# Moving memory scores behind a projection bank, and copies from VectorE to ScalarE, in a fused two-layer recurrent-memory kernel

## The chip, the cores and the metric

The kernel runs on one core of one Trainium2 chip. The metric is the device time of one execution in microseconds (us). Engines are called by their names or by their short forms in the profile: PE is TensorE (PEld its weight loads), DVE is VectorE, ACT is ScalarE, POOL is GpSimd, SP is SyncE.

## The reference

Two rounds of a segment-recurrent attention layer with memory tokens and a gated feed-forward layer, on 2048 tokens of width 448, in bfloat16:

```python
def _A_ref(x, mem0, Wq, Wk, Wv, Wo, seg_len):     # 64 segments of 32 tokens, 16 heads of 256
    mem = mem0                                    # 8 memory tokens
    for s in range(n_seg):
        h = concat([mem, x[:, s*seg_len:(s+1)*seg_len]], axis=1)   # 40 rows
        q, k, v = h@Wq, h@Wk, h@Wv
        scores = where(mask, q@k.T * Dh**-0.5, -1e9)
        o = (softmax(scores) @ v) @ Wo
        mem = o[:, :M]                            # the next segment's memory
        outs.append(o[:, M:])
    return concat(outs, axis=1)

def _B_ref(x, W_gate, W_up, W_down):
    gate, up = x@W_gate, x@W_up
    return (gate * (gate > 0) * up) @ W_down

x = A_x
x = x + _A_ref(layernorm(x), ...);  x = x + _B_ref(layernorm(x), ...)
x = x + _A_ref(layernorm(x), ...);  x = x + _B_ref(layernorm(x), ...)   # the same weights
```

## The kernel before, in words

**Folded weights.** A first part folds Wq with Wk and Wv with Wo for each head into resident tables, `A_sb` and `B_sb`. After it a head's scores are (h A) h' and its output (P h) B; keys and values are the rows of h themselves.

**Steps.** `step(g, ...)` is called for g = 0 to 68. It works on segment g of the first attention round (chain 0) and on segment g - 4 of the second one (chain 1) at the same time; both are active in steps 4 to 63. The two halves of the heads (hf 0 and 1, 8 heads each) go through it one behind the other. Every second step (g odd, from 3) also carries one block of feed-forward work, an object of class `Feed`, `ff`. I call a step with `ff` a long one and a step without it a short one.

**What a step does for a half.** `project` computes h A for 28 tiles of 128 columns, in five banks of PSUM, the on-chip memory of 8 banks that TensorE writes (`BANKS`: first tile and number of tiles; those at 0, 6, 12 and 18 have six tiles, that at 24 has four, and its upper and lower 64 partitions belong to different tiles). The copies out of the banks at 0, 6, 12 and 18 go to `TQ`, that at 24, the split bank, to `TZ` in two halves. In the profile these banks are `prj`. A quarter of the products of the four full banks is issued beforehand by `project_early`, so that 18 are left of each. `scores_m` computes the scores of the memory tokens' queries (bank `Sm`), `scores_x` those of the segments' own tokens (bank `Sx`); each sums over four parts of the width (kd 0 to 3: kd 0 and 1 read the TQ tiles 0 to 15, kd 2 the tiles 16 to 23, kd 3 reads TZ) and returns two functions from `softmax`. The first of them issues on VectorE the maximum (`mx`) and the difference (`se`) and on ScalarE the exponential; the second the sum (`ssum`), its reciprocal and the product, which gives `PM` or `PX`. `flipped` transposes those on TensorE (`pps`) and copies the result to SBUF (`PT`). `weigh_m` (banks `ya`, `yb`) and `weigh_x` (banks `y`) multiply it with h, held in `hk`, and copy to `Y`. `project_out` and `project_last` multiply Y by `B_sb` into `ox` and `o`; memory rows go back into h (`hT`) for the next step. The weigh_x of half 1 is called in the next step, through `late`.

**Order.** TensorE's instructions are issued in program order, and from the first step on so are VectorE's and ScalarE's (class `InOrder`). A planner, `bank`, gives every PSUM tile the bank that is free soonest by an estimate of time that it keeps while the program is written; a bank's new products wait for the last reader of its old ones.

**Around the change**, in a step with both chains, TensorE's order is: late weigh_x of half 1 of the step before (`y`), Sm of half 0, half 1's banks 0, 6, 24, 12, in a long step the transpose for the feed-forward layer (`tps`), bank 18, the flip of PM, Sx of half 0, `ya` and `yb` of half 0, Sm and Sx of half 1. A long step goes on with the gate and up products (`gate_up(u)`, u = 0 to 6: banks `ups` and `gps`, ScalarE's copy `ut`, VectorE's product `hh`; `ut` has two buffers), between which the flips of half 1's PM and half 0's PX stand, and with the down product (`down`). `ff.residual` and `ff.norm` add the residual (`xa`) and normalise (`xn`) on VectorE while half 0 is projected.

Of the kernel before, what the change touches and what calls it, by code (L numbers as in the profile page):

```python
# [40 lines left out]

BANKS = ((0, 6), (6, 6), (24, 4), (12, 6), (18, 6))
EARLY = (((0, 6), (12, 18)), ((0, 6), (12, 18)))


def upper(hf, t):

    return any(b <= t < b + 6 for _, b in EARLY[hf])

# [6 lines left out]
def build_kernel(ctx, tc, A_x, A_mem0, A_Wq, A_Wk, A_Wv, A_Wo, B_W_gate, B_W_up, B_W_down, out,  # L56
                 ntiles=16, nseg=64):
    nc = tc.nc
    P = nc.NUM_PARTITIONS
# [15 lines left out]
    def in_order(r):  # L75
        if last_pe[0] is not None:
            tc.add_manual_dep(r.ins, last_pe[0],
                              mybir.DependencyInfo(mybir.DependencyClass.NoSync,
                                                   mybir.DependencyReason.DATA),
                              reason="order of issue")  # L80
        last_pe[0] = r.ins.name
# [22 lines left out]
    dve, act = InOrder(nc.vector), InOrder(nc.scalar)  # L104
# [16 lines left out]
    def let_go(t):  # L121

        i, after = bank_of[t.name]
        held.discard(i)
        free_at[i] = now[0] + after
# [7 lines left out]
    def mm(out, lhsT, rhs, **k):  # L133
        in_order(nc.tensor.matmul(out, lhsT, rhs, **k))  # L134
        n = 1
        for d in out.shape[1:]:
            n *= d
        pair = lhsT.shape[0] <= 64 or lhsT.shape[-1] == 64 and out.shape[0] == 64
        passed(out, max(25, n / 2.4 + 2.5) * (0.5 if pair else 1))
# [5 lines left out]
    def evac(eng, dst, src):  # L145
        if eng is act:
            act.copy(dst, src)
        else:
            eng.tensor_copy(dst, src)
# [54 lines left out]
    TQ, TZ, YB, PX, PM = [], [], [], [], []  # L204
# [51 lines left out]
    with tc.tile_pool(name="pre", bufs=6) as pre:  # L256
# [71 lines left out]
        for p in range(NP):  # L328
            hf, p4 = divmod(p, 4)
# [31 lines left out]
        for p in range(NP):  # L361
            hf, p4 = divmod(p, 4)
# [4 lines left out]
            for eo in range(2):  # L367
                for kd in range(3):
                    bps = bank([P, 512], F32, "bps")
                    for t in range(2):  # L370
                        e = 2 * eo + t
                        mm(bps[:, 0:DM], vT[:, e, kd * 128:(kd + 1) * 128], wo[:, e, :],
                           start=(t == 0), stop=(t == 1))
# [4 lines left out]
            for t in range(2):  # L378
                for eo in range(2):
                    e = 2 * eo + t  # L380
                    mm(bps[64 * eo:64 * eo + 64, 0:DM], vT[:, e, 384:448], wo[:, e, :],
                       start=(t == 0), stop=(t == 1), tile_position=(0, 64 * eo))
# [115 lines left out]
    def moving(hb, j, idx, chains, rows=slice(0, P)):  # L498

        if len(chains) == 2:  # L500
            return hb[rows, j, idx * HI:(idx + 1) * HI].rearrange("p (c k) -> p c k", k=64)[:, :, 0:L]
        c = chains[0]
        return hb[rows, j, idx * HI + 64 * c:idx * HI + 64 * c + L]

    def project_early(hf, chains, hb, j):

        n = L * len(chains)
        pre = {}
        for pair in EARLY[hf]:
            for i0 in pair:  # L510
# [4 lines left out]
                       moving(hb, j, 3, chains, rows), start=(i == 0), stop=False, skip_group_check=True)  # L515
        return pre

    def project(hf, chains, hb, j, banks, pre={}, busy=False):

        n = L * len(chains)  # L520
        for i0, k in banks:
            ps = pre[i0] if i0 in pre else bank([P, 512], F32, "prj")
            for i in range(k):
                for kd in range(3 if i0 in pre else 4):
                    mm(ps[:, i * n:(i + 1) * n], A_sb[:, kd, hf, i0 + i, :], moving(hb, j, kd, chains),
                       start=(kd == 0 and i0 not in pre), stop=(kd == (2 if i0 in pre else 3)),
                       skip_group_check=i0 in pre)
            if i0 in pre:
                let_go(ps)
            if i0 < 24:  # L530
                T = TQ[hf][:].rearrange("p g u w -> p g (u w)")[:, :, 16 * i0:16 * (i0 + k)]
                parts = [(act if i0 % 12 or busy and hf and i0 else dve, slice(0, P), T)]
            else:
                parts = [(dve, slice(0, 64), TZ[hf][0:64, :, 0:64]),
                         (act, slice(64, 128), TZ[hf][64:128, :, 64:128])]
            for eng, rows, T in parts:
                T = T.rearrange("p g (t q) -> p t g q", q=16)
                if len(chains) == 2:
                    evac(eng, T, ps[rows, 0:k * n].rearrange("p (t g q) -> p t g q", t=k, q=16))
                    continue  # L540
                c = chains[0]
                src = ps[rows, 0:k * n].rearrange("p (t w) -> p t w", t=k)
                x, m = (0, SEG) if c == 0 else (MEM, 0)
                evac(eng, T[:, :, 2, MEM * c:MEM * c + MEM], src[:, :, m:m + MEM])
                evac(eng, T[:, :, 3 * c:3 * c + 2, :],
                     src[:, :, x:x + SEG].rearrange("p t (g q) -> p t g q", q=16))

    def queries(hf, g, kd):
        return TQ[hf][:, g, 2 * kd:2 * kd + 2, :] if kd < 3 else TZ[hf][:, g, :]
# [23 lines left out]

        return first, second

    def flipped(src, n, tag):
        pps = bank([P, n, 128], BF, "pps")
        for b in range(n):
            tr(pps[:, b, :], src[:, 2 * b:2 * b + 2, :], ident[:])
        PT = main.tile([P, n * 128], BF, tag=f"PT{tag}", name="PT")  # L580
        dve.tensor_copy(PT[:], pps[:].rearrange("p b q -> p (b q)"))
        return PT

    def active(g):
# [2 lines left out]
    def step(g, ff, pre, late):  # L587
        chains = active(g)
        xs = active(g - 1)
        ms = [c for c in chains if g - c * LAG + 1 < nseg]  # L590
        gb, j = divmod(g, BLK)
        hb = hTb[gb % 2]
# [22 lines left out]
        def scores_m(hf):  # L615
            if not ms:
                return (lambda: None,) * 2
            Sp = bank([P, 2, L], F32, "Sm", 1100)
            for kd in range(4):
                mm(Sp[:, :, :], queries(hf, 2, kd), moving(hb, j, kd, (0, 1)), start=(kd == 0), stop=(kd == 3))  # L620
            return softmax(Sp, 2, PM[hf], blk[:], f"m{hf}")

        def scores_x(hf):
            Sp = bank([P, 4, L], F32, "Sx", 2500 if hf == 0 else 3500 if ff is None else 8000)
            both = len(chains) == 2
            if not both:
                mm(Sp[:, :, :], ident[:], maskS[:], start=True, stop=False, skip_group_check=True)
            for half in range(2):
                for c in chains:
                    for kd in range(4):  # L630
                        mm(Sp[:, 2 * half + c, :], queries(hf, 3 * c + half, kd), moving(hb, j, kd, (c,)),
                           start=(both and kd == 0), stop=(kd == 3), skip_group_check=True)
            return softmax(Sp, 4, PX[hf], None, f"x{hf}", maskS[:] if len(chains) == 2 else None)

        def weigh_m(hf, hk, PT):
# [115 lines left out]
        if ff is not None:  # L751
            ff.residual()
        next_piece()
        project(0, chains, hb, j, BANKS[2:5], pre)
        if ff is not None:
            ff.norm()
        pre1 = {}
        if late is not None:
            pre1 = project_early(1, chains, hb, j)
            late()  # L760
        m0 = scores_m(0)
        m0[0]()
        project(1, chains, hb, j, BANKS[0:2], pre1)
        m0[1]()
        next_piece()
        project(1, chains, hb, j, BANKS[2:4], pre1, ff is not None)
        if ff is not None:
            ff.xposed()
        project(1, chains, hb, j, BANKS[4:5], pre1)
        pm = flipped(PM[0], 1, "m0") if ms else None  # L770
        x0 = scores_x(0)
        weigh_m(0, hk, pm)
        m1 = scores_m(1)
# [3 lines left out]
        if ff is not None:  # L777
            feed(0)
            m1[1]()
            feed(1)  # L780
            x0[1]()
            feed(2, 3)
            next_piece()
            pm = flipped(PM[1], 1, "m1") if ms else None
            feed(4)
            px0 = flipped(PX[0], 2, "x0")
            weigh_m(1, hk, pm)
            feed(5, 6)
            x1[0]()
            x1[1]()  # L790
            ox_open()
            project_out(0, 0, 8)
            next_piece()
            ff.down()
            ff.norm2()
            project_out(0, 8, NT)
            project_last()
            next_piece()
            project_out(1, 0, 12)
            px1 = flipped(PX[1], 2, "x1")  # L800
            ff.feed_on()
            project_out(1, 12, NT)
        else:
            next_piece()
            ox_open()
            m1[1]()
            x0[1]()
            project_out(0, 0, 23)
            pm = flipped(PM[1], 1, "m1") if ms else None
            project_out(0, 23, NT)  # L810
            px0 = flipped(PX[0], 2, "x0")
            weigh_m(1, hk, pm)
            x1[0]()
            next_piece()
            x1[1]()
            project_last()
            project_out(1, 0, 22)
            px1 = flipped(PX[1], 2, "x1")
            next_piece()
            project_out(1, 22, NT)  # L820
# [3 lines left out]
        pre = project_early(0, nxt, hTb[(g + 1) // BLK % 2], (g + 1) % BLK) if nxt else {}  # L824
# [7 lines left out]
    pre, late = {}, None  # L832
    for g in range(nsteps + 1):
# [3 lines left out]
        pre, late = step(g, Feed(i) if g % 2 and 0 <= i < nblk + LAG // BLK - 1 else None, pre, late)  # L837

    ff = Feed(nblk + LAG // BLK - 1)
# [64 lines left out]
```

## Time and profile before

| | |
|---|---|
| time, median of 3 runs | 1670.48 us (1670.42 to 1671.86) |
| time of the profiled execution | 1672.79 us |
| its span, first to last instruction | 1671.0 us |
| mean granted TensorE clock | 0.994 |
| busy: TensorE, VectorE, ScalarE | 97%, 73%, 41% |
| HBM traffic over the span | 15 GB/s |

The profile is that of one execution. Instructions are grouped by engine, operation and tile name; nearly all are issued through one helper for each kind of engine, so they share a few line numbers (L134 are matrix products and their weight loads, L142 transposes, L92 the instructions of VectorE and ScalarE), and the tile names tell them apart. A row of the order of time has start, duration, engine, operation, `out<-in`, and in brackets the idle time ahead of it with what ended it. Ends of products are modelled, since they overlap in the array.

### The profile page before, as it was taken

How to read it: one execution, taken by the hardware profiler on the slowest of the kernel's cores; microseconds unless marked ns; L12 is line 12 of the kernel's file. 1: busy time of each engine (PE TensorE's matmuls, PEld its weight loads, DVE VectorE, ACT ScalarE, POOL GpSimd, SP SyncE). 2: the span in 40 equal slices, each digit the busy share in tenths (PEclk: the TensorE clock that was granted, in tenths of full speed). 3: DMA queues.
4: the chain of work that ended last, by engine and by line, in shares of the span. 5: the costliest groups of instructions: out<-in, count | busy, mean ns of one | idle time of the engine just before them, and what ended most of it. 6: DMA issues, size and time to landing. Idle time of an engine off the chain costs nothing.

```text
span 1671.0 us, 90168 instructions
## 1 busy us (share of the span) xinstructions
PE 1614.8 (97%) x41152; PEld 1485.6 (89%) x41152; DVE 1212.2 (73%) x3984; ACT 689.0 (41%) x1998; POOL 90.9 (5%) x178
## 2 busy tenths in 40 slices
PE   8999999999999999999999999999999999999997
PEld 6698899999999899999999999999999999999886
DVE  7776777777777777777777777777777777777775
ACT  5733443444334434443344344433443344433432
POOL 6200000000000000000000000000000000000000
PEclk9989999999999999999999999999999999999999
DMA  9430000000000000000000000000000000000000
GB/s 253 129 108 15 8 9 9 4 9 9 9 9 9 9 9 6 7 9 9 9 9 9 9 9 4 9 9 9 9 9 9 9 4 9 9 7 7 6 6 6
DMA packets 26783, 33.16 MB, mean 20 GB/s; under 512 B 3352, under 2 KB 24736, under 8 KB 26400
## 3 DMA queue, kind: packets, MB, share of 16 engines
q1 hardware_dynamic: 25312, 23.70, 5.3%
q8 instruction: 322, 5.28, 1.3%
q0 software_dynamic: 1088, 3.68, 0.7%
q14 instruction: 61, 0.50, 0.1%
HBM read 23.70 MB, written 1.84 MB: 15 GB/s over the span
## 4 chain that ended last, share of the span: by engine, by line
PE 85%; DVE 7%; ACT 4%; POOL 2%; issue 1%; POOLq 0%; ACTq 0%; DVEq 0%
PE prj L134 24%; PE ox L134 24%; PE ups L134 6%; PE dps L134 5%; PE gps L134 5%; PE o L134 5%; PE Sx L134 3%; PE y L134 3%; ACT Y L92 2%; PE Sm L134 2%; PE ya L134 2%; PE bps L134 1%; DVE stats L92 1%; PE pps L142 1%; ACT TQ L92 1%
## 5 line engine op out<-in xcount | busy, mean ns | idle before, releaser
L134 PE MATMUL prj<-hT,A_sb 128*128 128x80 bf16 (+3 forms) x15232 | 530.2, 199 | 0.2 <-issue 0.2
L134 PEld LDWEIGHTS <-A_sb 128*128 128x128 bf16 (+1 forms) x15232 | 493.8, 99 | 16.2 <-issue 0.9
L134 PEld LDWEIGHTS <-B_sb 128*128 128x128 bf16 (+1 forms) x15232 | 491.1, 103 | 14.0 <-issue 0.4
L134 PE MATMUL ox<-Y,B_sb 128*128 128x80 bf16 (+4 forms) x11424 | 435.9, 199 | 0.4 <-issue 0.4
L92 DVE CAST Y<-y 128x256 bf16<-128x256 f32 (+2 forms) x400 | 160.9, 457 | 66.2 <-PE y L134 66.2
L92 ACT CAST TQ<-prj 128x480 bf16<-128x480 f32 (+1 forms) x340 | 162.2, 498 | 86.6 <-PE prj L134 84.6
L92 ACT ACTIVATE se<-se 128x80 f32<-128x80 f32 (+1 forms) x270 | 81.9, 303 | 212.2 <-DVE se L92 212.2
L92 DVE CAST TQ<-prj 128x480 bf16<-128x480 f32 (+2 forms) x268 | 150.1, 569 | 6.3 <-PE prj L134 5.7
L134 PEld LDWEIGHTS <-hk 40*128 40x128 bf16 (+1 forms) x1950 | 105.6, 96 | 44.7 <-issue 31.9
L134 PE MATMUL ups<-xT,Wu_sb 128*128 128x128 bf16 (+1 forms) x1904 | 140.8, 217 | 1.9 <-DVE hh L92 1.3
L134 PE MATMUL gps<-xT,Wg_sb 128*128 128x128 bf16 (+1 forms) x1904 | 140.9, 218 | 0.0
L92 ACT CAST Y<-y 128x256 bf16<-128x256 f32 (+1 forms) x368 | 129.6, 418 | 20.5 <-PE y L134 16.5
L92 DVE SCALAR_TENSOR_TENSOR hh<-gps,ut 128x256 bf16<-128x256 f32 (+1 forms) x238 | 93.8, 406 | 59.7 <-PE gps L134 53.2
L92 ACT CAST ut<-ups 128x256 bf16<-128x256 f32 (+1 forms) x238 | 81.8, 358 | 89.0 <-DVE hh L92 52.7
L134 PEld LDWEIGHTS <-Wu_sb 128*128 128x128 bf16 x1904 | 111.2, 99 | 2.4 <-issue 2.4
L134 PEld LDWEIGHTS <-Wg_sb 128*128 128x128 bf16 x1904 | 112.7, 99 | 0.0
L134 PEld LDWEIGHTS <-TQ 128*128 128x128 bf16 x1938 | 86.8, 97 | 27.4 <-issue 11.8
L92 DVE COPY PT<-pps 128x128 bf16<-128x128 bf16 (+1 forms) x270 | 68.7, 254 | 49.5 <-PE pps L142 48.1
L134 PE MATMUL y<-PT,hk 40*128 40x256 bf16 (+1 forms) x1280 | 99.3, 248 | 4.0 <-ACT Y L92 0.6
L218 POOL TENSOR_SCALAR rstd<-mv 128x1 f32<-128x1 f32 x67 | 14.8, 221 | 1516.2 <-DVE mv L92 1516.2
L92 ACT CAST TZ<-prj 64x320 bf16<-64x320 f32 (+2 forms) x152 | 55.9, 378 | 98.7 <-DVE TZ L92 96.5
L134 PE MATMUL dps<-Wd_sb,hh 128*128 128x448 bf16 x476 | 96.2, 354 | 0.0
(117 smaller groups left out, 1924.9 us busy)
## 6 DMA issues: line engine op xcount, KB each, us to landing
wo<-in_A_Wo_dram POOLq DMA_DIRECT2D x8, 448.0 KB, 5.7
nat<-in_A_Wq_dram SPq DMA_DIRECT2D x8, 384.0 KB, 6.1
nat<-in_A_Wk_dram SPq DMA_DIRECT2D x8, 384.0 KB, 5.6
nat<-in_A_Wv_dram SPq DMA_DIRECT2D x8, 384.0 KB, 5.0
xa<-in_A_x_dram SPq DMA_DIRECT2D x32, 56.0 KB, 2.2
xa<-xp SPq DMA_DIRECT2D x32, 56.0 KB, 1.9
out_dram<-xa SPq DMA_DIRECT2D x32, 56.0 KB, 2.3
xp<-in_A_x_dram SPq DMA_DIRECT2D x30, 56.0 KB, 2.6
```

Of the source, the lines that this page charges most:

```text
L92: r = f(*a, **k)
L134: in_order(nc.tensor.matmul(out, lhsT, rhs, **k))
L142: in_order(nc.tensor.transpose(out, src, idn))
L218: nc.gpsimd.tensor_scalar(out=rstd[:], in0=mv[:, 1:2], scalar1=EPS, scalar2=None, op0=ALU.add)
```

## The change

Five edits, all in the steps:

1. In a step, half 0's `scores_m` and the first part of its softmax come behind half 1's first bank (the bank at 0) instead of ahead of it. The second part of that softmax is issued between the products of the bank at 6 and the copy out of it (`first`), instead of behind that copy.
2. In long steps both halves of the split bank (24) are copied by ScalarE, for both halves of the heads; before, VectorE took one.
3. In long steps, of half 1's banks the one at 0 is copied by ScalarE and the one at 6 by VectorE; before it was the other way round. Those at 12 and 18 stay on ScalarE.
4. In long steps the flip of half 1's PM and that of half 0's PX are copied by ScalarE instead of VectorE.
5. The scores sum over kd in the order 0, 1, 3, 2, so that the part that reads the bank at 18 comes last.

```diff
+KD = (0, 1, 3, 2)
...
-    def project(hf, chains, hb, j, banks, pre={}, busy=False):
+    def project(hf, chains, hb, j, banks, pre={}, busy=False, first=None):
...
             if i0 in pre:
                 let_go(ps)
+            if first is not None:
+                first()
             if i0 < 24:
...
-                parts = [(act if i0 % 12 or busy and hf and i0 else dve, slice(0, P), T)]
+                parts = [(act if (i0 != 6 if busy and hf else i0 % 12) else dve, slice(0, P), T)]
             else:
-                parts = [(dve, slice(0, 64), TZ[hf][0:64, :, 0:64]),
+                parts = [(act if busy else dve, slice(0, 64), TZ[hf][0:64, :, 0:64]),
                          (act, slice(64, 128), TZ[hf][64:128, :, 64:128])]
...
-    def flipped(src, n, tag):
+    def flipped(src, n, tag, eng=dve):
...
-        dve.tensor_copy(PT[:], pps[:].rearrange("p b q -> p (b q)"))
+        evac(eng, PT[:], pps[:].rearrange("p b q -> p (b q)"))
...
-            for kd in range(4):
-                mm(Sp[:, :, :], queries(hf, 2, kd), moving(hb, j, kd, (0, 1)), start=(kd == 0), stop=(kd == 3))
+            for kd in KD:
+                mm(Sp[:, :, :], queries(hf, 2, kd), moving(hb, j, kd, (0, 1)), start=(kd == KD[0]), stop=(kd == KD[-1]))
...
-        project(0, chains, hb, j, BANKS[2:5], pre)
+        project(0, chains, hb, j, BANKS[2:5], pre, ff is not None)
...
+        project(1, chains, hb, j, BANKS[0:1], pre1, ff is not None)
         m0 = scores_m(0)
         m0[0]()
-        project(1, chains, hb, j, BANKS[0:2], pre1)
-        m0[1]()
+        project(1, chains, hb, j, BANKS[1:2], pre1, ff is not None, m0[1])
         next_piece()
         project(1, chains, hb, j, BANKS[2:4], pre1, ff is not None)
         if ff is not None:
             ff.xposed()
-        project(1, chains, hb, j, BANKS[4:5], pre1)
+        project(1, chains, hb, j, BANKS[4:5], pre1, ff is not None)
...
-            pm = flipped(PM[1], 1, "m1") if ms else None
+            pm = flipped(PM[1], 1, "m1", act) if ms else None
             feed(4)
-            px0 = flipped(PX[0], 2, "x0")
+            px0 = flipped(PX[0], 2, "x0", act)
```

More of the change, by code (lines that the diff above doesn't have):

```diff
@@ L629, in scores_x @@
                 for c in chains:
-                    for kd in range(4):
+                    for kd in KD:
                         mm(Sp[:, 2 * half + c, :], queries(hf, 3 * c + half, kd), moving(hb, j, kd, (c,)),
-                           start=(both and kd == 0), stop=(kd == 3), skip_group_check=True)
+                           start=(both and kd == KD[0]), stop=(kd == KD[-1]), skip_group_check=True)
             return softmax(Sp, 4, PX[hf], None, f"x{hf}", maskS[:] if len(chains) == 2 else None)
```

## The prediction

> **What bounds the kernel now.** I read the page first (busy shares), then the waits, the stretches of one pair of steps, and the order of time of that pair on four engines.
>
> The page's engine row, the list of waits (engine line waited for: us in total, times, longest) and the table by stretch (a step without feed-forward work, here a short step, then one with it, a long step):
>
> ```profile
> PE 1614.8 (97%) x41152; PEld 1485.6 (89%) x41152; DVE 1212.2 (73%) x3984; ACT 689.0 (41%) x1998; POOL 90.9 (5%) x178
> ...
> PE ya L134 <- DVE PT L92: 14.2, 37, 0.6
> PE Sm L134 <- ACT Y L92: 13.3, 36, 0.4
> ...
> 719.53:738.12 18.59, 18.19 (x532) 17.54 (x530) 14.14 (x48) 7.96 (x23) 0.00 (x0) 1.00 0.01 4
> 738.12:766.98 28.86, 28.21 (x668) 25.82 (x667) 20.63 (x66) 11.51 (x33) 1.58 (x4) 1.00 0.05 11
> ```
>
> TensorE, in order, is the bound: 97% busy, clock 1.00, 18.59 us for a short step and 28.86 us for a long one. Only its pauses can be won, and there are few. Two have a name: it waits some 36 times for ScalarE's copy out of a bank (Sm <- ACT Y) and 37 times for VectorE's copy of a flip (ya <- DVE PT), about 0.4 us each. VectorE is 76% busy in a short step (14.14 of 18.59), 71% in a long one; ScalarE 40%.
>
> Where these pauses lie in a short step (start us, us, engine, what; the bracket is idle time and its releaser):
>
> ```profile
> 724.54 0.65 PE L134 MATMUL y<-PT,hk 40*128 40x256 bf16 x10
> 725.59 0.27 PE L134 MATMUL Sm<-hT,TQ 128*128 128x80 bf16 x3 [0.40 <-ACT Y L92]
> 725.73 3.32 PE L134 MATMUL prj<-hT,A_sb 128*128 128x80 bf16 x88
> 728.89 0.22 PE L142 MATMUL pps<-ident,PM 128*128 128x128 bf16 x1
> 729.42 0.27 PE L134 MATMUL ya<-PT,hk 128*128 128x128 bf16 x2
> 724.96 1.03 ACT L92 CAST Y<-y 128x512 bf16<-128x512 f32 x3 [0.20 <-PE y L134]
> 726.67 0.27 ACT L92 ACTIVATE se<-se 128x80 f32<-128x80 f32 x1 [0.68 <-DVE se L92]
> 724.99 1.22 DVE L92 CAST Y<-y 128x512 bf16<-128x512 f32 x3 [0.77 <-PE y L134]
> 726.13 0.23 DVE L92 TENSOR_REDUCE mx<-Sm 128x2 f32<-128x80 f32 x1
> 726.39 0.24 DVE L92 TENSOR_TENSOR se<-Sm,mx 128x80 f32<-128x80 f32 x1
> 726.58 0.66 DVE L92 CAST TQ<-prj 128x480 bf16<-128x480 f32 x1
> 727.16 0.23 DVE L92 TENSOR_REDUCE ssum<-se 128x2 f32<-128x80 f32 x1
> 728.44 0.66 DVE L92 CAST TQ<-prj 128x480 bf16<-128x480 f32 x1
> 729.14 0.23 DVE L92 COPY PT<-pps 128x128 bf16<-128x128 bf16 x1
> ```
>
> Sm takes the bank that the first y product used, and waits until ScalarE has emptied it. But VectorE, from its first Y copy at 724.99 to the flip's copy at 729.14, has no bracket: it works through without a pause, and ya comes right behind that copy. So this 0.40 us of TensorE is nearly covered by VectorE.
>
> The same place in a long step, and its second half:
>
> ```profile
> 742.34 0.45 DVE L92 CAST TZ<-prj 64x320 bf16<-64x320 f32 x1
> 742.88 0.42 ACT L92 CAST TZ<-prj 64x320 bf16<-64x320 f32 x1 [1.01 <-DVE TZ L92]
> 743.32 0.56 ACT L92 CAST TQ<-prj 128x480 bf16<-128x480 f32 x1
> 743.35 0.96 PE L134 MATMUL y<-PT,hk 40*128 40x256 bf16 x10
> 743.93 0.20 PEld L134 LDWEIGHTS <-hk 40*128 40x128 bf16 x4 [0.37 <-issue]
> 744.46 0.27 PE L134 MATMUL Sm<-hT,TQ 128*128 128x80 bf16 x3
> 745.06 0.23 DVE L92 TENSOR_REDUCE mx<-Sm 128x2 f32<-128x80 f32 x1
> 747.88 1.02 ACT L92 CAST TQ<-prj 128x480 bf16<-128x480 f32 x2
> 748.51 0.27 PE L134 MATMUL ya<-PT,hk 128*128 128x128 bf16 x2
> 748.73 0.43 PE L134 MATMUL Sm<-hT,TQ 128*128 128x80 bf16 x3
> 749.03 0.24 PE L134 MATMUL Sx<-hT,TQ 128*128 128x40 bf16 x3
> 749.24 0.24 DVE L92 TENSOR_REDUCE mx<-Sm 128x2 f32<-128x80 f32 x1
> 753.01 0.22 PE L142 MATMUL pps<-ident,PM 128*128 128x128 bf16 x1
> 753.08 0.37 ACT L92 CAST ut<-ups 128x256 bf16<-128x256 f32 x1 [0.78 <-DVE hh L92]
> 753.71 0.75 DVE L92 SCALAR_TENSOR_TENSOR hh<-gps,ut 128x256 bf16<-128x256 f32 x2
> 754.37 0.21 DVE L92 COPY PT<-pps 128x128 bf16<-128x128 bf16 x1
> 754.64 0.27 PE L134 MATMUL ya<-PT,hk 128*128 128x128 bf16 x2 [0.41 <-DVE PT L92]
> ```
>
> There are three pauses. From y to Sm 1.11 us go by (743.35 to 744.46) where the ten y products alone take 0.65: the residual and its statistics hold VectorE, so its half of the split bank is late (742.34), ScalarE's half waits 1.01 us for it, the last query copy ends only at 743.88, and y's second bank is the one it empties (weight load at 743.93, 0.37 us idle). At 748.73 the second Sm takes 0.30 us instead of the 0.14 of the first (725.59 to 725.73), because ScalarE is still copying the last query bank (747.88 + 1.02 = 748.90). At 754.64 ya waits 0.41 us for a flip whose transpose had been issued at 753.01, but whose copy stood in VectorE's queue behind two hh.
>
> **Short steps: a small loss.** Sm goes behind 18 products of half 1's first bank. One takes (728.89 - 725.73) / 88 = 36 ns, so 0.65 us, and by 725.84 its bank has long been emptied (724.96 plus one of three copies in 1.03): the 0.40 us goes. What is late next is VectorE. Its order becomes TQ, mx, se, ssum, where it was mx, se, TQ, ssum: the 0.58 us slot of TQ (726.58 to 727.16) had covered the exponential. Now TQ starts at 726.13, mx at 726.71, se at 726.97 and ends at 727.21; the exponential follows in 0.04 (as 726.63 to 726.67), takes 0.27, and ssum starts 0.04 behind it at 727.56 instead of 727.16. VectorE idles 0.35 us and everything queued behind ssum (the mask product, PM, the split bank's half, the last TQ) is 0.40 later; ScalarE's half of the split bank waits with it. The flip's copy had 0.12 us of room (VectorE free at 728.44 + 0.58 = 729.02, copy at 729.14), so ya moves from 729.42 to 729.70: **+0.28 us**, while TensorE gets there at about 729.0 and pauses 0.7. Behind ya products and copies follow in the old distances. Between the ends: nothing, if VectorE filled the gap, and +0.40 with no room at all; I keep 0.28, since the row of VectorE has no bracket. [...]
>
> **Long steps, first half: a gain.** With both halves of the split bank on ScalarE its copies no longer wait for VectorE: ScalarE was free at 741.87 (742.88 - 1.01), so two of 0.42 us end near 742.8, and the last query copy can start when TensorE delivers it, which in the short step is 0.34 us ahead of y (the second row is used below):
>
> ```profile
> 724.20 0.56 ACT L92 CAST TQ<-prj 128x480 bf16<-128x480 f32 x1 [0.35 <-PE prj L134]
> 747.53 0.42 DVE L92 COPY xT<-tps 128x512 bf16<-128x512 bf16 x1 [0.19 <-PE tps L142]
> ```
>
> So it runs from 743.01 to 743.57 and y takes its undisturbed 0.65. Bank 0 and Sm follow without a pause: TensorE is ahead by 1.11 - 0.65 = **0.46 us**. Checked against the other engines: VectorE reaches mx at 745.06 as before, at the latest, since only the TZ half has gone from ahead of it; without TQ and TZ in between, and with the exponential uncovered, ssum is at 745.92, PM near 746.6, then the swapped copy (bank 6) 0.58 and xT (its copy of 0.42), so VectorE is free at 747.7 for the flip, whose transpose ends at 747.74. ya moves the full 0.46 to 748.05. ScalarE: Y to 744.84, TQ bank 0 to 745.41, the exponential (se ends 745.57) to 745.9, two halves of 0.42 from 746.2 to 747.1, bank 12 to 747.64, bank 18 from 747.72 (TensorE's end) to 748.28. The second Sm, now with that bank last, needs it at about 748.38, so its extra 0.15 us goes too. What follows hangs on VectorE's mx (749.24), which comes behind the Y copy of ya and so moves to 748.70: **0.54 us** for this half, not 0.61. In the feed part ScalarE's and VectorE's turns (ut, hh, the next ups bank) all follow from there.
>
> **Long steps, second half: a gain.** The flip's copy goes to ScalarE behind the ut of 753.08, which ends at 753.45. I take 0.25 us for it, between these rows of ScalarE's copies of bf16 out of a bank, near the first:
>
> ```profile
> L92 ACT COPY hk<-kps 128x64 bf16<-128x64 bf16 x68 | 15.1, 222 | 4.0 <-DVE hk L92 1.3
> L92 ACT COPY hT<-tps 128x256 bf16<-128x256 bf16 x32 | 11.9, 372 | 51.5 <-DVE hT L92 51.5
> ```
>
> It ends near 753.7 in the old times, and ya would be reached at 754.23 (754.64 - 0.41): the **0.41 us** go, and even 0.37 us would hide. The bank that ya takes is freed by the first of the two hh (753.71 + 0.42), just in time. [...] The flip of the token scores (0.37 us at most) has no reader until the next step's start. Swapping banks 0 and 6 and the order of the last bank cost nothing by themselves: as many products and copies, and room of 0.07 us at the flip.
>
> **Sum.** The loop has 30 steps of each kind with both layers active; the other nine I leave unchanged, give or take 2 us. Short +0.28, long -0.54 - 0.41 = -0.95, a pair -0.67: 30 x -0.67 = -20.1 us. The profiled execution took 1672.79 us (span 1671.0 and 1.8 around it), so 1652.7 for such a one; it lay 2.3 us above the median of the runs, 1670.48, against which I forecast **1650.4 us**. No DMA or queue of SP and GpSimd moves.
>
> **Rivals.** *The short steps lose nothing:* something behind ssum has room that I don't see. Then -28.5 us, **1642**. For: ya's 0.06 us behind PT is tight already, and little would be needed; against: VectorE's unbroken rows. Chance 0.16.
>
> *ScalarE becomes late in the long step:* between mx and the second Sm it gets two TZ and three TQ copies, and my room there is 0.1 us. Each further delay reaches Sm one for one; half a microsecond takes 15 us back: **1665**. [...] Chance 0.18.
>
> *Slower:* the exponential of the long step now stands behind ScalarE's copy of bank 0 in its queue. Up to 0.1 us late is free; beyond that ssum, PM, the bank-6 copy, xT and the flip all slide and ya with them. At 0.7 us late the pair breaks even; one microsecond late (a copy of 0.56 and one of 0.42 more in front of it) gives +0.33 a pair: **1680**. The order of issue puts only bank 0 there, so 0.08. That the reordering wins nothing, because Sm still finds its bank full, would leave the short steps' loss alone (1679); by the times above the bank is empty 0.3 us before, so 0.02.
>
> **Numbers.** My forecast has 0.56, the rivals 0.16, 0.18, 0.08 and 0.02. Its own range is 1643 to 1658 (short 0 to 0.40; long 0.75 to 1.1). Taking in the first rival and the second up to its price gives 1637 to 1665. A difference of 0.2%, 3.3 us, is what the runs can tell: faster 0.87, same 0.04, slower 0.09.
>
> **What would show it.** Right: Sm <- ACT Y gone from the waits; ya <- DVE PT no longer in long steps but in short ones, 0.7 us each; ssum <- ACT se (VectorE idle) up by 0.3 us a step; short steps near 18.9 us, long near 27.9. Wrong: short steps at 18.59 or below (first rival), Sm waiting for ACT TQ in the long step (second), or ya waiting for DVE PT in both kinds (slower).

## The result, and the profile after

The changed kernel takes 1645.78 us (median of four runs, 1644.08 to 1647.7) against 1670.45 of the kernel before beside it: a ratio of 0.9853, 95% interval 0.9836 to 0.987. It is 24.7 us faster; the forecast was 20.1.

The page of the changed kernel (span and engines), its waits, and the table by stretch of one long and one short step, each from its first early products to those of the next:

```profile
span 1643.8 us, 90068 instructions
...
PE 1604.2 (98%) x41152; PEld 1479.4 (90%) x41152; DVE 1171.7 (71%) x3847; ACT 722.9 (44%) x2135; POOL 90.9 (6%) x178
...
DVE ssum L95 <- ACT se L95: 54.2, 135, 0.7
PE ya L137 <- DVE PT L95: 15.9, 37, 0.5
...
727.19:755.07 27.88, 27.88 (x668) 25.72 (x667) 19.52 (x62) 12.66 (x37) 1.58 (x4) 1.00 0.04 11
755.07:773.83 18.76, 18.30 (x532) 17.52 (x530) 14.01 (x48) 7.85 (x23) 0.00 (x0) 1.00 0.02 4
```

A long step is 0.98 us shorter (28.86 before), a short one 0.17 longer (18.59), a pair 0.81 shorter. Thirty pairs make 24.3 us, beside 24.7 between the medians. (The two profiled executions lie 27.2 us apart; some 2.4 of that come in the first and last four steps and outside the steps, which the prediction left unchanged, give or take 2 us.) In a long step TensorE is now busy from end to end; in a short one 0.46 us are left idle. Sm <- ACT Y has gone from the waits. ya <- DVE PT stands there as often as before (37 times), but in the short steps instead of the long ones, as the order of time shows. A short step of the changed kernel (TensorE's rows, then VectorE's; here and below rows are picked out of the order of time, and those between them are left out):

```profile
760.08 0.65 PE L137 MATMUL y<-PT,hk 40*128 40x256 bf16 x10
761.32 0.24 PE L137 MATMUL Sm<-hT,TQ 128*128 128x80 bf16 x2
764.04 0.23 PE L145 MATMUL pps<-ident,PM 128*128 128x128 bf16 x1
765.13 0.27 PE L137 MATMUL ya<-PT,hk 128*128 128x128 bf16 x2 [0.46 <-DVE PT L95]
...
760.54 1.22 DVE L95 CAST Y<-y 128x512 bf16<-128x512 f32 x3 [0.78 <-PE y L137]
761.67 0.65 DVE L95 CAST TQ<-prj 128x480 bf16<-128x480 f32 x1
762.24 0.23 DVE L95 TENSOR_REDUCE mx<-Sm 128x2 f32<-128x80 f32 x1
763.08 0.23 DVE L95 TENSOR_REDUCE ssum<-se 128x2 f32<-128x80 f32 x1 [0.34 <-ACT se L95]
763.90 0.48 DVE L95 CAST TZ<-prj 64x320 bf16<-64x320 f32 x1
764.30 0.64 DVE L95 CAST TQ<-prj 128x480 bf16<-128x480 f32 x1
764.87 0.21 DVE L95 COPY PT<-pps 128x128 bf16<-128x128 bf16 x1
```

The 0.40 us at Sm are gone, VectorE waits 0.34 us for the exponential, and TensorE, which issued the transpose at 764.04, waits for VectorE's copy of it. From y to ya it takes 5.05 us, where it took 4.88.

A long step of the changed kernel (ScalarE, TensorE and VectorE, in order of time):

```profile
730.82 0.88 ACT L95 CAST TZ<-prj 64x320 bf16<-64x320 f32 x2
732.15 0.56 ACT L95 CAST TQ<-prj 128x480 bf16<-128x480 f32 x1 [0.45 <-PE prj L137]
732.42 0.71 PE L137 MATMUL y<-PT,hk 40*128 40x256 bf16 x10
733.72 0.24 PE L137 MATMUL Sm<-hT,TQ 128*128 128x80 bf16 x2
734.74 0.27 ACT L95 ACTIVATE se<-se 128x80 f32<-128x80 f32 x1 [0.26 <-DVE se L95]
736.17 1.24 ACT L95 CAST TQ<-prj 128x480 bf16<-128x480 f32 x2
737.13 0.27 PE L137 MATMUL ya<-PT,hk 128*128 128x128 bf16 x2
737.35 0.24 PE L137 MATMUL Sm<-hT,TQ 128*128 128x80 bf16 x2
737.78 0.23 DVE L95 TENSOR_REDUCE mx<-Sm 128x2 f32<-128x80 f32 x1
741.89 0.27 ACT L95 COPY PT<-pps 128x128 bf16<-128x128 bf16 x1
742.72 0.28 PE L137 MATMUL ya<-PT,hk 128*128 128x128 bf16 x2
```

The last query copy starts 0.27 us ahead of y and waits only for TensorE; y has no pause, Sm follows behind the first bank, ScalarE ends the last query copy at 737.41, just as the second Sm needs it, and the second ya finds its flip copied 0.56 us earlier (742.16).

### The profile page after: what moved, and what is told of

It is laid out like the page before. It is cut to its first block, busy times and chain, and to the rows that moved or that the text cites. A ratio compares the mean times of both kernels' runs of the same rounds, so it can differ in the third digit from the quotient of the medians.

```text
span 1643.8 us, 90068 instructions
## 1 busy us (share of the span) xinstructions
PE 1604.2 (98%) x41152; PEld 1479.4 (90%) x41152; DVE 1171.7 (71%) x3847; ACT 722.9 (44%) x2135; POOL 90.9 (6%) x178
## 4 chain that ended last, share of the span: by engine, by line
PE 86%; DVE 11%; POOL 2%; ACT 1%; issue 1%; POOLq 0%; ACTq 0%
PE ox L137 24%; PE prj L137 23%; PE ups L137 6%; PE gps L137 6%; PE dps L137 5%; PE o L137 5%; PE y L137 4%; DVE Y L95 3%; DVE TQ L95 2%; PE Sx L137 2%; PE ya L137 2%; PE bps L137 1%; PE pps L145 1%; DVE rs L95 1%; PE kps L145 1%; PE yb L137 1%
## 5 line engine op out<-in xcount | busy, mean ns | idle before, releaser
L137 PE MATMUL prj<-hT,A_sb 128*128 128x80 bf16 (+3 forms) x15232 | 540.0, 199 | 0.3 <-issue 0.2
L95 DVE TENSOR_REDUCE ssum<-se 128x2 f32<-128x80 f32 (+1 forms) x270 | 73.9, 274 | 54.2 <-ACT se L95 54.2
L95 ACT CAST TZ<-prj 64x320 bf16<-64x320 f32 (+1 forms) x224 | 83.5, 382 | 57.5 <-DVE TZ L95 46.1
L95 ACT COPY os<-o 64x16 f32<-64x16 f32 (+3 forms) x135 | 25.7, 190 | 167.4 <-PE o L137 165.8
L137 PE MATMUL y<-PT,hk 40*128 40x256 bf16 (+1 forms) x1280 | 94.1, 248 | 0.9 <-ACT Y L95 0.6
```

Source lines behind the costliest of these rows:

```text
L95: r = f(*a, **k)
```

## The experiments

Theory of the pauses: an edit is worth what TensorE waits at the place that it relieves, after the next queue in line has had its say. Rival: what counts is how much work VectorE is relieved of. Each run had the kernel before beside it, with medians from 1668.85 to 1670.45 us, so a difference between two medians of the table is good to some 1.6 us; the step lengths are sharper. Step lengths are those of the middle of each trace, from one step's `o` products to the next one's: "short" from a long step's to the short step's behind it, "long" from there on.

| kernel | median, us | ratio to before, 95% | short | long |
|---|---|---|---|---|
| before | 1670.45 | | 18.75 | 28.70 |
| changed | 1645.78 | 0.9853 (0.9836 to 0.987) | 18.92 | 27.71 |
| flips_only | 1655.72 | 0.9911 (0.9894 to 0.9927) | 18.75 | 28.23 |
| split_only | 1666.14 | 0.9976 (0.9967 to 0.9985) | 18.75 | 28.60 |
| order_only | 1695.28 | 1.0151 (1.0135 to 1.0167) | 18.95 | 29.21 |
| no_swap | 1654.75 | 0.9908 (0.9894 to 0.9923) | 18.92 | 28.06 |
| no_kd | 1645.51 | 0.9855 (0.9842 to 0.9869) | 18.96 | 27.71 |
| no_split | 1682.93 | 1.0075 (1.0058 to 1.0092) | 18.92 | 28.89 |
| no_order | 1651.23 | 0.9891 (0.9874 to 0.9907) | 18.75 | 28.18 |
| old_in_short | 1638.97 | 0.9815 (0.9802 to 0.9828) | 18.75 | 27.70 |
| cover | 1630.47 | 0.9766 (0.9753 to 0.978) | 18.49 | 27.71 |
| split_short | 1631.77 | 0.9775 (0.9762 to 0.9789) | 18.52 | 27.70 |
| cover_split | 1624.91 | 0.9728 (0.9714 to 0.9743) | 18.29 | 27.70 |

### One edit alone, on the kernel before

**flips_only**

```diff
-            pm = flipped(PM[1], 1, "m1") if ms else None
+            pm = flipped(PM[1], 1, "m1", act) if ms else None
...
-            px0 = flipped(PX[0], 2, "x0")
+            px0 = flipped(PX[0], 2, "x0", act)
```

> The kernel before with only the two flips' copies of a long step on ScalarE. Theory of the pauses (a copy is worth what TensorE waits for it): the 0.41 us pause at ya in the feed part goes in some 30 long steps and nothing else changes, 12 us, 1658 (1656 to 1661); no ya <- DVE PT pauses of that kind are left. Rival (the gain is VectorE's relief, in proportion to the busy time moved: 0.5 of 1.4 us of a long step, of 24.7 us in all): 9 us, 1662. If ScalarE gets to the copy late, under 5 us.

14.2 us faster than its kernel before (1669.87), just beyond the range expected, a long step 0.47 us shorter. The waits of this run:

```profile
PE Sm L134 <- ACT Y L92: 16.5, 59, 0.4
PE ya L134 <- DVE PT L92: 1.4, 5, 0.3
```

The pause at ya is gone from the long steps and nothing took its place. The 23 additional entries at Sm are no new pause: they are the 0.15 us ahead of Sm in long steps, which are as long in the kernel before, where most of them are just too short to be listed. The gain is a little over the 0.41 us of the bracket; the weight load for ya had stood idle for 0.53. It is more than the rival's 9 us.

**split_only**

```diff
-                parts = [(dve, slice(0, 64), TZ[hf][0:64, :, 0:64]),
+                parts = [(act if busy else dve, slice(0, 64), TZ[hf][0:64, :, 0:64]),
...
-        project(0, chains, hb, j, BANKS[2:5], pre)
+        project(0, chains, hb, j, BANKS[2:5], pre, ff is not None)
```

> The kernel before with only both halves of the split bank on ScalarE in long steps. Theory of the pauses: the second y bank is no longer late, but Sm still stands in its old place and waits for ScalarE's first Y copy until about 744.40 instead of 744.46 in the old times, so of the 0.46 us only 0.06 goes, and some 0.1 at the second Sm: 5 us, 1665 (1662 to 1668). Rival (VectorE's relief, 0.9 of 1.4 us moved): 16 us, 1655.

3.7 us faster, 0.10 us a long step, far from the rival's 16. The wait for the y bank moved on to Sm, which in long steps now waits 0.40 us, as in short ones, where it was 0.15 (the waits of this run, 36 times and 13.3 us before, and a long step):

```profile
PE Sm L134 <- ACT Y L92: 23.8, 59, 0.4
...
742.42 0.27 PE L134 MATMUL Sm<-hT,TQ 128*128 128x80 bf16 x3 [0.40 <-ACT Y L92]
```

**order_only**: the diff's lines of `step` and the `first` of `project` alone, with the old engines.

> The kernel before with only the memory scores moved behind half 1's first bank, in all steps, every copy on its old engine and the old order over kd. Theory of the pauses: a short step loses 0.17 us as in the changed kernel; in a long step the pause at Sm goes but the one at y stays, and with the bank at 0 on VectorE the exponential is uncovered there too, so that VectorE's half of the split bank, ScalarE's half behind it and the last query copy are late and the second Sm waits some 0.5 us: slower by 8 to 16 us, 1678 to 1686. Rival (the pauses at Sm <- ACT Y are free time: 13.3 us of it): faster by up to 13 us, 1657 to 1665.

25.4 us slower: the direction was expected, the size not. A short step is 0.20 us longer, a long one 0.51. A long step of this run, the second Sm on TensorE and what it waits for (VectorE's sum and its half of the split bank, ScalarE's half, ScalarE's last two query copies):

```profile
709.42 0.20 PE L134 MATMUL Sm<-hT,TQ 128*128 128x80 bf16 x1
709.83 0.21 PE L134 MATMUL Sm<-hT,TQ 128*128 128x80 bf16 x1 [0.21 <-ACT TQ L92]
710.29 0.21 PE L134 MATMUL Sm<-hT,TQ 128*128 128x80 bf16 x1 [0.25 <-ACT TQ L92]
...
707.38 0.24 DVE L92 TENSOR_REDUCE ssum<-se 128x2 f32<-128x80 f32 x1 [0.40 <-ACT se L92]
708.21 0.48 DVE L92 CAST TZ<-prj 64x320 bf16<-64x320 f32 x1
708.77 0.42 ACT L92 CAST TZ<-prj 64x320 bf16<-64x320 f32 x1 [0.98 <-DVE TZ L92]
709.22 1.02 ACT L92 CAST TQ<-prj 128x480 bf16<-128x480 f32 x2
```

The uncovered exponential (0.40 us ahead of ssum) delays VectorE's half to 708.21, ScalarE sits 0.98 us idle behind it, and the second Sm's four products take 0.95 us (709.42 to about 710.37) where they took 0.30. I had allowed some 0.5 us for this place. The pause at Sm <- ACT Y was no free time.

### One edit left out of the changed kernel

**no_swap**

```diff
-                parts = [(act if (i0 != 6 if busy and hf else i0 % 12) else dve, slice(0, P), T)]
+                parts = [(act if i0 % 12 or busy and hf and i0 else dve, slice(0, P), T)]
```

> The changed kernel with the banks at 0 and 6 of half 1 on their old engines in long steps (0 on VectorE, 6 on ScalarE). Theory of the pauses: the exponential is then uncovered late and ScalarE's queue (exponential, bank 6, two halves, banks 12 and 18) runs 0.5 us or more behind TensorE, so that the second Sm waits 0.5 to 0.7 us a long step: 15 to 21 us slower than the changed kernel, 1661 to 1667. Rival (the same number of copies on each engine, so no difference): within 3 us of it, 1643 to 1649.

9.0 us slower than the changed kernel (1645.78), 0.35 us a long step: about midway between the two expectations and outside both. The mechanism is the theory's, the size is not: the second Sm waits where it was said, for less:

```profile
740.73 0.21 PE L137 MATMUL Sm<-hT,TQ 128*128 128x80 bf16 x1 [0.22 <-ACT TQ L95]
```

**no_split**

```diff
-                parts = [(act if busy else dve, slice(0, 64), TZ[hf][0:64, :, 0:64]),
+                parts = [(dve, slice(0, 64), TZ[hf][0:64, :, 0:64]),
```

> The changed kernel with the split bank's first half back on VectorE in long steps, all else as changed. Theory of the pauses (the edits hang together): y's second bank is late again (0.37 us), and in half 1 the first half now stands on VectorE behind the bank at 6, so that ScalarE's half and its two query copies behind it end about 1 us later than the second Sm needs them, and xT and the flip are later too: 1.2 us a long step or more, 36 us slower than the changed kernel, 1675 to 1690, slower than the kernel before. Rival (the edits add up; alone this one was worth 3.7 us): 1648 to 1651.

37 us slower than the changed kernel and 13 slower than the one before, as worked out. In a long step of this run y takes 0.96 us again, ScalarE sits 1.99 us idle for VectorE's half, and the second Sm waits twice:

```profile
751.84 0.42 ACT L95 CAST TZ<-prj 64x320 bf16<-64x320 f32 x1 [1.99 <-DVE TZ L95]
...
747.08 0.96 PE L137 MATMUL y<-PT,hk 40*128 40x256 bf16 x10
752.90 0.21 PE L137 MATMUL Sm<-hT,TQ 128*128 128x80 bf16 x1 [0.21 <-ACT TQ L95]
753.36 0.21 PE L137 MATMUL Sm<-hT,TQ 128*128 128x80 bf16 x1 [0.22 <-ACT TQ L95]
```

An edit worth 3.7 us alone is worth 37 among the others: single values don't add up. By step lengths the three single edits make -0.47, -0.10 and +0.71 us a pair, +0.14 if they added up. no_swap has these three together, with only the order over kd besides, and its pair is 0.47 shorter; all five make -0.82.

**no_kd** (`KD = (0, 1, 2, 3)`)

> The changed kernel with the scores summed in the old order 0, 1, 2, 3. In the changed kernel ScalarE ends the last query copy at 737.41 and the second Sm of the long step starts at 737.35, so with the part that needs that copy third instead of fourth it waits some 0.04 us more a long step: 0 to 2 us slower than the changed kernel, 1645 to 1648. If the order were what took the 0.15 us pause of before away: 4.5 us slower, 1650.

1645.51: no difference that the runs can tell. A short step is 0.04 us longer; in a long one the second Sm takes the 0.04 us more that were expected, but the step is as long as in the changed kernel.

**no_order**

```diff
-        project(1, chains, hb, j, BANKS[0:1], pre1, ff is not None)
         m0 = scores_m(0)
         m0[0]()
-        project(1, chains, hb, j, BANKS[1:2], pre1, ff is not None, m0[1])
+        project(1, chains, hb, j, BANKS[0:2], pre1, ff is not None)
+        m0[1]()
```

> The changed kernel with the memory scores in their old place in all steps, all else as changed. Theory of the pauses: in a long step Sm then waits for ScalarE's first Y copy, which ends about 1.07 us behind the start of y, 0.4 to 0.46 us a step; a short step wins back its 0.17 us. A pair is 0.25 to 0.3 us longer, 8 to 9 us slower than the changed kernel, 1652 to 1656. If the reordering is worth nothing in long steps either: 5 us faster than it, 1641.

1651.23: 5.5 us slower than the changed kernel by the medians, just below the range expected, and 6.3 by the two ratios. The steps do what was said: long +0.47, short -0.17, so 30 pairs make 9; in the two traces the first and last four steps, where not all of the work is active, give 2.5 of it back. The long step's pause is back:

```profile
735.40 0.23 PE L137 MATMUL Sm<-hT,TQ 128*128 128x80 bf16 x2 [0.40 <-ACT Y L95]
```

### The short steps

**old_in_short**: the changed kernel with the old place of the scores where `ff is None`.

> The changed kernel with the old place of the memory scores in short steps. If the reordering costs a short step 0.17 us: short steps are back at 18.59 us and the kernel takes 5 us less, 1641 (1639 to 1643). If it is worth something in short steps too: slower than the changed kernel.

1638.97, 6.8 us less than the changed kernel, at the lower edge of the range, short steps back at the old length. The reordering costs short steps the 0.17 us that it was thought to, 5.1 us in thirty; the edit also reaches steps without feed-forward work at the ends of the loop, where about 1 us more comes from.

**cover**

```diff
+        else:
+            m0 = []
+
+            def scores_first():
+                m0.extend(scores_m(0))
+                m0[0]()
+
+            project(1, chains, hb, j, BANKS[0:1], pre1, False, scores_first)
```

> The changed kernel, but in short steps the scores, maximum and difference of half 0 are issued between the products and the copy of half 1's first bank, so that VectorE's order is again maximum, difference, copy, sum while TensorE keeps the new order. If the uncovered exponential is what short steps lose: VectorE is 0.37 us earlier at the flip, TensorE waits at ya 0.2 us instead of 0.55, short steps take about 18.4 us instead of 18.76: 11 us faster than the changed kernel, 1635 (1632 to 1638). If something else holds ya: no change, 1646.

1630.47, 15.3 us less than the changed kernel, more than the 11 expected. A short step is 0.43 us shorter, 12.9 us in thirty; most of the rest comes in the steps at the ends of the loop. A short step of this run, VectorE, ScalarE's exponential and TensorE in order of time:

```profile
708.37 0.24 DVE L95 TENSOR_TENSOR se<-Sm,mx 128x80 f32<-128x80 f32 x1
708.53 0.65 DVE L95 CAST TQ<-prj 128x480 bf16<-128x480 f32 x1
708.65 0.27 ACT L95 ACTIVATE se<-se 128x80 f32<-128x80 f32 x1 [0.69 <-DVE se L95]
709.10 0.22 DVE L95 TENSOR_REDUCE ssum<-se 128x2 f32<-128x80 f32 x1
710.30 0.64 DVE L95 CAST TQ<-prj 128x480 bf16<-128x480 f32 x1
710.40 0.22 PE L145 MATMUL pps<-ident,PM 128*128 128x128 bf16 x1
710.87 0.21 DVE L95 COPY PT<-pps 128x128 bf16<-128x128 bf16 x1
711.13 0.27 PE L137 MATMUL ya<-PT,hk 128*128 128x128 bf16 x2
```

ssum has no bracket: the copy covers the exponential again, while TensorE keeps the new order and the 0.40 us at Sm stay won. So the uncovered exponential is the cause of the short steps' loss, shown and not only argued. Of the 0.43 us, 0.36 lie between the transpose and ya (1.09 us apart in the changed kernel, 0.73 here) and 0.07 ahead of the transpose, which no longer has to wait for PM. ya still comes later than the 0.53 us behind the transpose that it took in the kernel before (728.89 to 729.42), since VectorE copies the bank at 12 first.

**split_short**: `act if busy or hf` for the first half of the split bank.

> The changed kernel with both halves of half 1's split bank on ScalarE in short steps too. If VectorE's queue is what ya waits for in short steps: it is relieved of 0.40 us ahead of the flip and ya comes 0.35 to 0.40 us earlier, 10 to 12 us faster than the changed kernel, 1634 to 1636, short steps about 18.4 us. If ScalarE's half and last query copy become late instead (the second Sm waits): under 5 us.

1631.77, 14.0 us less than the changed kernel, again more than expected, short steps 0.40 us shorter (12 us in thirty, about 2 more at the ends of the loop): relieving VectorE by one copy ahead of the flip does nearly as much as covering the exponential.

**cover_split**: both.

> The changed kernel with the two repairs of short steps together: the scores issued ahead of the first bank's copy, and both halves of half 1's split bank on ScalarE. Each alone left ya 0.16 to 0.20 us behind what the transpose allows. If that rest is VectorE's queue too: ya comes 0.53 us behind the transpose, as in long steps, 5 us faster than either alone, 1624 to 1627, short steps 18.3 us from o to o (18.49 and 18.52 alone). If the two relieve the same thing only once: 1630.

1624.91, 20.9 us less than the changed kernel and 45.0 less than the one before beside it (ratio 0.9728, 0.9714 to 0.9743): the best version found. The flip's way in a short step of this run:

```profile
709.56 0.22 PE L145 MATMUL pps<-ident,PM 128*128 128x128 bf16 x1
710.10 0.27 PE L137 MATMUL ya<-PT,hk 128*128 128x128 bf16 x2
```

0.54 us from transpose to ya without a bracket, as in long steps and as in short steps of the kernel before (0.53): here TensorE's own order is the limit.

## Why the prediction was right, point by point

- **What bounds it.** Right: TensorE's pauses, and VectorE's queue as what nearly covers the one at Sm in short steps.
- **Short steps.** Direction and mechanism right, size too large: +0.17 us instead of +0.28. VectorE waits 0.34 us for the exponential (0.35 worked out): it starts nothing between se (762.50 + 0.24) and ssum (763.08). In the kernel before it waited in the same way at the sum of the token scores, 0.40 and 0.46 us (DVE ssum <- ACT se: 29.4 us, 68 times). ssum is 0.37 us later against its Y copies (763.08 - 760.54 to 727.16 - 724.99), 0.40 worked out. The term that was off is the room behind it, 0.12 us: from the split bank's half to the copy behind it (the bank at 12) VectorE now takes 0.40 us (763.90 to 764.30), where the old rows had 0.47 (727.97 to 728.44). The old 0.07 us were a wait for TensorE that shows no bracket. Counted back from the flip's transpose at 728.89, with 18 products of the bank at 18 between, the last product of the bank at 12 starts at 728.21 and by its modelled end is done at 728.41; the copy starts 0.04 us behind that, in each of 27 short steps in the middle of the trace, and 0.8 us behind it in the changed kernel. So "works through without a pause" was not quite true of VectorE, and the room was 0.19 us; the last 0.04 of the difference are spread over several rows. The pause at ya is 0.46 us where 0.7 was forecast.
- **Long steps, first half.** Right: y to ya is 4.71 us (737.13 - 732.42) against 5.16, 0.45 less (0.46 worked out); VectorE's next mx comes 5.36 us behind y against 5.89, 0.53 less (0.54). ScalarE's queue held as worked out: its last query copy ends 4.99 us behind the start of y, 4.93 in the working.
- **Long steps, second half.** Right: y to the second ya is 10.30 us against 11.29, so 0.99 in all, 0.95 worked out. ScalarE's copy of the flip took 0.27 us, 0.25 expected; a straight line between the prediction's own two rows (222 ns for 64, 372 for 256) gives 0.27.
- **The sum.** -0.67 us a pair forecast, -0.81 measured: 0.11 of the 0.14 is the short step's term. The time lies inside the range and inside the forecast's own range of 1643 to 1658. That narrower range is not what its stated ends add up to: short 0 to 0.40 and long 0.75 to 1.1 give 1637 to 1660. The total alone would not decide, since 1645.78 lies 3.8 us from the first rival's 1642 and 4.6 from 1650.4; the step lengths do.
- **Rivals.** "The short steps lose nothing" fell: they lose 0.17 us, and old_in_short and cover give it back. Its reason, room behind ssum that was not seen, was true of 0.07 us. "ScalarE becomes late in the long step" is not what the changed kernel does, but it is near: leaving out the swap (+0.35 us a long step) or the split bank (+1.18) brings it on at the place named, the second Sm. "Slower" did not come: the exponential started 2.32 us behind y where 2.26 was worked out. Missed: that the order over kd is worth nothing measurable; the prediction gave it a share of the 0.15 us at the second Sm, but no_kd, with the old order, has long steps as short as the changed kernel's.
- **Not foreseen in the prediction:** how much the edits depend on each other. The reordering alone makes the kernel 25 us slower.

## What to carry to other kernels

Before you move an instruction out of a wait on the bounding engine, lay the next queue over the same stretch: where its rows stand without a bracket, the wait is nearly covered (here the 0.40 us at Sm, without which short steps were 0.17 us longer), and the order of that queue (here, what stands between the exponential's input and its sum) decides. A missing bracket is no proof of an unbroken queue: compare the distance between two starts with the same pair elsewhere, which here showed 0.07 us of hidden room. When a reordering frees one engine, look at which copy used to fill the other engine's wait for a third, and keep it there. Judge such edits together and by leaving one out, since one alone can cost what the set gains (here the reordering alone 25.4 us, the set 24.7).

## What was not expected of the hardware

Nothing of its behaviour; one price is worth keeping. The groups of flips' copies in the changed kernel (busy us in all, mean ns of one, idle before):

```profile
L95 DVE COPY PT<-pps 128x256 bf16<-128x256 bf16 x103 | 30.0, 291 | 39.1 <-PE pps L145 39.0
L95 DVE COPY PT<-pps 128x128 bf16<-128x128 bf16 x102 | 22.0, 216 | 0.2 <-PE pps L145 0.2
L95 ACT COPY PT<-pps 128x256 bf16<-128x256 bf16 x33 | 12.5, 378 | 0.0
L95 ACT COPY PT<-pps 128x128 bf16<-128x128 bf16 x32 | 8.7, 272 | 0.0
```

ScalarE takes 272 and 378 ns where VectorE takes 216 and 291: dearer by 56 and 87 ns. It was still the better place in the long steps, where two hh stood ahead of the copy in VectorE's queue (flips_only, 14.2 us).
